# The first quad's softmax in two halves of 256 columns, with a new table of order and other counts of filler matmuls

## The chip, the core and the metric

The kernel runs on one core of one Trainium2 chip. Its time is device microseconds (us) of that core for one launch. Three runs of the kernel before gave a median of 709.91 us (709.32 to 710.12).

A core has TensorE (PE in the rows; PEld is its weight load), VectorE (DVE), ScalarE (ACT), GpSimd (POOL) and SyncE (SP), which here only issues transfers. A "q" behind a name (SPq) is an engine's sequencer. Each engine works through its own list in order and waits on semaphores for the others.

## The reference

Attention between 512 tokens and 32 state rows in each of 32 heads, in both directions, then two MLPs over the 2176 rows that come out, all in float32:

```python
scores = scale * x @ state.T                 # per head: x 512x64, state 32x64
a = softmax(scores);  xread = a @ state      # (a /= sum + 1e-09)
a2 = softmax(scale * state @ x.T);  sread = a2 @ x
x = concatenate([xread, sread], axis=2)      # heads side by side: 512 wide
h = x @ w_in;  g = where(h >= 1, h, where(h <= -1, 0, (h + 1) ** 2 / 4))
x = g @ w_out                                # first MLP, 2048 wide
return (x @ w_a * (x @ w_b)) @ w_out         # second MLP, 1536 wide
```

The weights arrive as 64-bit numbers and are brought to float32 on the chip.

## The kernel before

**Stages.** The first stage computes the attention and the first half of the first MLP; the second, h = g @ w_out in a seven-product scheme over quarter blocks; the third, the second MLP in the same scheme. Every large product is computed from operands that are split into a high and a low part, as three matmuls on a pair of 128-row blocks (`three`, L407). The stage around the change lasts until some 140 us; its matmuls and nearly all others are issued on line L401 (`mms`).

**The first stage.** Heads are taken four at a time: a "quad" is four heads, and a pair of quads is one of the four batches. For quad k, `a_qk` (L631) multiplies scores into bank 4 or 5 (in the rows `first`, later one tile `lower`), for quad 0 in two halves of 256 columns as its tokens land. `a_soft` (L655) is the softmax in eleven steps, each on 512 columns: transpose and maximum on DVE, subtraction on POOL, exponential on ACT, sum, a small addition and the reciprocal on DVE, multiplication on POOL, transpose back on DVE, the high part on ACT (`hi_of`, L381) and the low part on DVE (L683). The other direction is `s_soft` (L736), `s_tr` (L783: transposes on TensorE) and `s_read` (L802: the product with the tokens `xn`, 32 small matmuls for each quad, quad 0 first).

**State times weights.** Instead of attention times state and then times w_in, state times w_in is computed once for each batch and each quarter n of w_in (`w_steps`, L694; PE line L704 into the tile `upper`), then split by one copy on ACT (L376) and one subtraction on DVE (L386). After that one **unit** of six matmuls of 512 columns (`h_mm`, L853) gives 128 of the 2048 hidden columns for one batch. Units 0 to 3 of batch 0 use quarter 0, units 4 to 7 quarter 1, and so on. A `gate` (L829: two ACT steps, one of them at times on POOL, and DVE at L847) turns a unit into g, which is stored to DRAM.

**Weights.** Each pair of blocks of w_in is 1 MB as loaded (`conv_steps`, L420). It is turned into float32 by three steps, each on DVE, POOL or ACT: copy (L451 on ACT, L453 elsewhere), byte (L457 on ACT, L459 elsewhere) and join (L470, always DVE).

**What sets the order.** All this is recorded as a list of operations. `Flow.order` (L98) then lists them with assumed durations and due times; the table `NUDGE` (L20) shifts single operations' due times by numbers, and takes an engine from some. SP issues the loads in that order, and they are carried in one queue. The start alone is written out by hand, in `phase_one`: after `s0` and `s1`, the steps of quads 0 and 1, a row of named steps whose order on DVE, ACT and POOL is kept (`flow.row`).

**Fillers.** A filler is a 128 by 128 float32 matmul of a constant, whose result is not used (L908). Ten of zeros stand at the start (`WARM`), ten ahead of the first state product and ten behind it (`FILL`), and `Flow.order` puts some ahead of operations that begin a bank anew, when by its own reckoning PE would be idle after the first 13 us (`SPAN`).

Of the kernel before, what the change touches and what calls it, by code (L numbers as in the profile page):

```python
# [9 lines left out]
F32 = mybir.dt.float32  # L10
# [7 lines left out]


NUDGE = {  # L20
    2: (-37,), 44: (39,), 49: (0.5, "POOL"), 68: (160.5,), 74: (20,), 91: (-0.5,), 99: (24.5, "POOL"), 100: (13,),
    105: (18,), 110: (33,), 118: (94.5,), 133: (10.5,), 134: (17,), 135: (32,), 146: (2413,), 187: (27, "POOL"),
    219: (0, "POOL"), 260: (2,), 316: (2,), 790: (-14.5,), 1015: (-9,), 1070: (-7,), 1097: (1,), 1105: (-3.5,),
    1110: (2,), 1142: (-7,), 1215: (3,), 1229: (-7.5,), 1248: (2,), 1257: (-2,),
}


class Flow:
# [9 lines left out]
    DMA_FROM = 1.1  # L38

    EARLY, SOON = 26.0, 0.3  # L40
    FULL, SPARE, FILLER, SPAN = 0.75, 0.4, 0.23, (13.0, 60.0)

    def __init__(self):
        self.ops = []
        self.last = {}
        self.readers = {}
        self.loose = set()
        self.gate = None
        self.hold = None
# [5 lines left out]
        self.fresh, self.fill = set(), {}  # L55
        self.psum = {}

    def op(self, engs, emit, rd=(), wr=(), size=0, loose=False, port=False):
        i = len(self.ops)
        if port:  # L60
            self.port.add(i)
        self.hurry[i] = self.rush
        if loose:
            self.loose.add(i)
        self.psum[i] = {b - b % 2 if b > 3 else b for s, lo, hi in [*rd, *wr] if s == "P" for b in range(lo, hi)}
        deps = set()
        last, readers = self.last, self.readers
# [12 lines left out]
        for c in cells(list(wr) + shut):  # L80
            if c in last:
                deps.add(last[c])
            deps.update(readers.pop(c, ()))
            last[c] = i
        if self.gate is not None and size:
            deps.add(self.gate)
        if self.hold is not None:
            deps.add(self.hold)
        e = next(iter(engs))
        if self.row is not None and len(engs) == 1 and e in ("DVE", "ACT", "POOL"):  # L90
            if e in self.row:
                deps.add(self.row[e])
            self.row[e] = i
        deps.discard(i)
        self.ops.append((engs, emit, sorted(deps), size))
        return i

    def order(self):  # L98
# [101 lines left out]
        for i in use:  # L200
            if self.ops[i][4] != "PE" or start[i] > self.SPAN[1]:
                continue
            best = (0, 0)
            for b in (0, 1, 2, 3, 4, 6):
                on = [x for x in use if b in self.psum[x]]
                at = next((k for k, x in enumerate(on) if (start[x], x) >= (start[i], i)), None)
                if at is not None and on[at] in self.fresh:
                    t = max([f] + [fin[x] for x in on[:at]])
                    best = max(best, (int(self.FULL * (start[i] - t - self.SPARE) / self.FILLER), b))
            if best[0] > 0 and start[i] > self.SPAN[0]:  # L210
                self.fill[i] = best
# [6 lines left out]
def attention_then_two_mlps(  # L218
# [13 lines left out]
    nc = tc.nc  # L232
# [136 lines left out]
    def eng(e):  # L369
        return {"DVE": nc.vector, "POOL": nc.gpsimd}[e]  # L370
# [278 lines left out]
    def g32(t):  # L649
        return t.rearrange("p (a n) -> p a n", n=NS)  # L650

    def b32(t):
        return t.unsqueeze(2).to_broadcast([P, 16, NS])

    def a_soft(k, sub=("POOL",), mult=("POOL",), low=("DVE", "POOL")):  # L655
        d = qs[k]
        t1, b = d["t1"], sbank[k]
        mx, sm = d["sm"].sub(16, 16), d["sm"].sub(32, 16)
        hi, lo = att[k]

        def spread(engs, alu, v):
            op(
                {x: {"DVE": 0.7, "POOL": 1.05}[x] for x in engs},
                lambda e: eng(e).tensor_tensor(g32(t1()), g32(t1()), b32(v()), alu),
                regs(t1, v),
                regs(t1),
                port=True,
            )

        return [  # L670
            lambda: op({"DVE": 0.72}, lambda e: nc.vector.transpose(t1(), banks[b]), [bank(b)], regs(t1)),
            lambda: op({"DVE": 0.69}, lambda e: nc.vector.reduce_max(mx(), g32(t1()), axis=AX.X), regs(t1), regs(mx)),
            lambda: spread(sub, ALU.subtract, mx),
            lambda: act(t1, t1, 512, AF.Exp, regs(t1), regs(t1), scale=SCALE),
            lambda: op({"DVE": 0.69}, lambda e: nc.vector.reduce_sum(sm(), g32(t1()), axis=AX.X), regs(t1), regs(sm)),
            lambda: plus_tiny(mx, d["sm"].sub(32, 32), 16),
            lambda: op({"DVE": 0.25}, lambda e: nc.vector.reciprocal(mx(), mx()), regs(mx), regs(mx)),
            lambda: spread(mult, ALU.mult, mx),
            lambda: op({"DVE": 0.71}, lambda e: nc.vector.transpose(d["at"](), t1()), regs(t1), regs(d["at"])),
            lambda: hi_of(hi, d["at"], 512, regs(d["at"]), regs(hi)),  # L680
            lambda: op(
                {x: {"DVE": t_tt(512), "POOL": 1.05}[x] for x in low},
                lambda e: eng(e).tensor_tensor(lo(), d["at"](), hi(F32), ALU.subtract),  # L683
                regs(d["at"], hi),
                regs(lo),
                port=True,
            ),
        ]
# [721 lines left out]
    def phase_one():  # L1410
# [23 lines left out]
        tr, mx, sub, exp, sm, eps, rec, mult, back, high, low = range(11)  # L1434
        copy, byte, join = range(3)
        prod, top, rest, top1, rest1 = range(5)
        warm(FILL[0])
# [233 lines left out]
```

## Time and profile before

| | |
|---|---|
| median of three runs | 709.91 us (709.32 to 710.12) |
| profiled execution, its own time | 709.89 us |
| its span, first to last instruction | 708.1 us |
| PE busy | 697.8 us, 99% of the span |
| DVE, ACT, POOL busy | 554.6, 419.1, 110.2 us |
| moved by DMA | 128.93 MB |

What follows comes from that one execution; 1.8 us of its own time lie outside of the span. The page's share of an engine is a mean over all stages. "The chain that ended last" is followed from the last instruction back, at each step to what released it. In a timeline row the number in brackets is how long the engine had been idle, and the arrow names what ended that.

### The profile page before, as it was taken

To read this page: it belongs to the slowest core of one execution; us is meant where nothing else is said; L and a number is where in the kernel's file an instruction comes from. 1 tells how busy PE (TensorE), PEld (TensorE's weight loads), DVE (VectorE), ACT (ScalarE), POOL (GpSimd) and SP (SyncE) were. 2 spreads that over 40 slices of the span, in tenths; PEclk is the share of its full clock that TensorE was granted. 3 is DMA by queue.
4 is the path that set the end of the run, shared out by engine and by line. 5 is a ranking of instruction groups with operands and counts; after the bars stand their busy time and mean duration, and the time that the engine had idled before them with its cause. 6 is when DMAs were issued, how large, how long until landed. Compare 5 with 4: busy or idle time off the path is not lost.

```text
span 708.1 us, 12274 instructions
## 1 busy us (share of the span) xinstructions
PE 697.8 (99%) x4834; PEld 657.1 (93%) x4834; DVE 554.6 (78%) x702; ACT 419.1 (59%) x626; POOL 110.2 (16%) x76
## 2 busy tenths in 40 slices
PE   7899999999999999999999999999999999999998
PEld 6666677989999999999999999999999999999998
DVE  7897898899996787899998686756636889986761
ACT  5689888787444455666576576465325545544440
POOL 3564858873000000000000000000000000000000
PEclk9999999999999999999999999999999999999999
DMA  8978879596583165151445767362731358454201
GB/s 311 407 254 308 290 260 293 166 321 202 193 285 118 63 198 189 48 192 65 135 149 180 239 223 245 120 222 76 235 112 42 98 156 286 141 161 138 87 32 45
DMA packets 75994, 128.93 MB, mean 182 GB/s; under 512 B 5664, under 2 KB 52000, under 8 KB 75936
## 3 DMA queue, kind: packets, MB, share of 16 engines
q1 hardware_dynamic: 75664, 128.01, 53.8%
q8 instruction: 38, 0.62, 0.4%
q14 instruction: 20, 0.16, 0.1%
q10 hardware_dynamic: 272, 0.13, 0.1%
HBM read 84.87 MB, written 43.25 MB: 181 GB/s over the span
## 4 chain that ended last, share of the span: by engine, by line
PE 93%; DMA 3%; DVE 3%; issue 0%; ACT 0%; SPq 0%; ACTq 0%; DVEq 0%
PE bank L401 86%; PE bank L885 2%; PE upper L704 2%; DMA fs<-in_xn_dram 2%; DMA fs<-in_xt_dram 1%; PE lower L812 1%; DMA f<-in_w_dram 1%; PE first L812 0%; DVE f L964 0%; DVE r L386 0%; PE lower L791 0%; DVE fs L470 0%; PE lower L581 0%; DVE rh L386 0%; ACT rh L376 0%
## 5 line engine op out<-in xcount | busy, mean ns | idle before, releaser
L401 PE MATMUL bank<-rh,r 128*128 128x352 f32 (+2 forms) x1398 | 222.6, 315 | 0.0
L401 PEld LDWEIGHTS bank<-rh,r 128*128 128x128 f32 x1398 | 215.8, 189 | 1.0 <-DVE rh L386 0.7
L376 ACT ACTIVATE f<-bank 128x368 f32<-128x368 f32 (+3 forms) x183 | 82.6, 453 | 124.9 <-PE bank L401 122.9
L401 PE MATMUL bank<-r,r 128*128 128x368 f32 (+1 forms) x960 | 156.2, 315 | 0.0
L401 PEld LDWEIGHTS bank<-r,r 128*128 128x128 f32 x960 | 147.9, 188 | 0.0
L376 ACT ACTIVATE rh<-f 128x736 fp32r<-128x736 f32 (+5 forms) x120 | 100.4, 846 | 72.3 <-PE bank L401 62.4
L386 DVE TENSOR_TENSOR f<-bank,f 128x368 f32<-128x368 f32 (+2 forms) x170 | 86.1, 514 | 70.7 <-PE bank L401 59.7
L386 DVE TENSOR_TENSOR rh<-f,rh 128x736 fp32r<-128x736 f32 (+5 forms) x120 | 117.0, 984 | 28.2 <-ACT rh L376 28.0
L401 PE MATMUL bank<-r 128*128 128x512 f32 (+1 forms) x582 | 119.4, 358 | 0.4 <-DVE r L683 0.4
L401 PEld LDWEIGHTS bank<-r 128*128 128x128 f32 x582 | 94.6, 189 | 24.6 <-issue 4.2
L386 DVE TENSOR_TENSOR r<-f,r 128x768 fp32r<-128x768 f32 (+6 forms) x85 | 96.0, 1139 | 16.4 <-ACT r L376 16.0
L376 ACT ACTIVATE r<-f 128x768 fp32r<-128x768 f32 (+6 forms) x85 | 80.2, 953 | 37.5 <-PE bank L401 17.3
L401 PE MATMUL bank<-rh 128*128 128x352 f32 (+2 forms) x564 | 93.4, 318 | 0.2 <-DVE f L386 0.2
L964 DVE TENSOR_TENSOR f<-f 128x256 f32<-128x256 f32 (+7 forms) x108 | 86.4, 818 | 6.9 <-DMA f<-p_d 4.9
L401 PEld LDWEIGHTS bank<-rh 128*128 128x128 f32 x564 | 88.4, 189 | 1.4 <-issue 0.5
L401 PE MATMUL bank<-r,rh 128*128 128x368 f32 (+1 forms) x480 | 80.3, 315 | 0.0
L401 PEld LDWEIGHTS bank<-r,rh 128*128 128x128 f32 x480 | 74.3, 188 | 0.0
L451 ACT ACTIVATE f<-f 128x512 fp8e5<-128x512 fp8e5 (+1 forms) x31 | 32.2, 1040 | 23.4 <-DMA f<-in_w_dram 17.9
L470 DVE SCALAR_TENSOR_TENSOR f<-f 128x1024 uint32<-128x1024 uint32 (+1 forms) x34 | 36.5, 1072 | 6.4 <-ACT f L457 6.4
L457 ACT ACTIVATE f<-f 128x512 fp8e5<-128x512 f32 (+1 forms) x35 | 37.3, 1067 | 0.7 <-POOL f L453 0.3
L833 ACT ACTIVATE f<-bank,half 128x512 f32<-128x512 f32 x40 | 27.1, 683 | 7.3 <-PE bank L401 3.1
L842 POOL TENSOR_TENSOR f<-f 128x512 f32<-128x512 f32 x20 | 27.5, 1384 | 22.4 <-ACT f L833 16.9
(76 smaller groups left out, 438.8 us busy)
## 6 DMA issues: line engine op xcount, KB each, us to landing
f<-in_w_dram SPq DMA_DIRECT2D x25, 1024.0 KB, 6.2
f<-g_d SPq DMA_DIRECT2D x36, 368.0 KB, 5.0
f<-p_d SPq DMA_DIRECT2D x17, 768.0 KB, 5.1
g_d<-f SPq DMA_DIRECT2D x40, 256.0 KB, 4.2
f<-in_w_dram SPq DMA_DIRECT2D x18, 512.0 KB, 4.1
p_d<-f SPq DMA_DIRECT2D x48, 184.0 KB, 2.1
g_d<-fs SPq DMA_DIRECT2D x28, 256.0 KB, 4.8
f<-g_d SPq DMA_DIRECT2D x16, 352.0 KB, 4.9
```

What stands on the lines that cost most here:

```text
L376: lambda e: nc.scalar.activation(dst(), src(), func, **{k: (v() if callable(v) else v) for k, v in kws.items()}),
L386: op({"DVE": t_tt(n)}, lambda e: nc.vector.tensor_tensor(dst(), a(), b(), alu), rd, wr, port=port)
L401: nc.tensor.matmul(o, w, x, start=first and k == 0, stop=last and k == n - 1, skip_group_check=onto)
L451: nc.scalar.activation(to(), of(), AF.Copy, saturate=False)
L457: nc.scalar.activation(to(), z(), AF.Copy, saturate=False)
L470: lambda e: nc.vector.scalar_tensor_tensor(out(U32), words_of(1, U32)(), 5, z(U32), ALU.logical_shift_right, ALU.bitwise_or),
L704: nc.tensor.matmul(banks[ab[q]][o : o + NS, :cols].rearrange("p (f x) -> p f x", x=P), st[q]()[64 * h : 64 * h + 64, NS * j : NS * j + NS] ...
L812: nc.tensor.matmul(banks[4][64 * e2 : 64 * e2 + 64, o : o + NS], xn()[:, c * 256 + p * 128 + e2 * 64 : c * 256 + p * 128 + (e2 + 1) * 64], ...
L833: lambda e: nc.scalar.activation(g(), h(), AF.Relu, bias=half[:, 0:1], scale=0.5),
L842: eng(e).tensor_tensor(g(), g(), g(), ALU.mult)
L885: nc.tensor.matmul(banks[b][:, P * i : P * i + P], w[:, P * c : P * c + P], xs()[:, P * c : P * c + P], start=c == 0, stop=c == 3,)
L964: lambda e: eng(e).tensor_tensor(dst(), a(), b(), alu),
```

## The change

`a_soft` takes a `part`: with 0 or 1 it does steps one to ten on 256 of the 512 columns (8 groups of 32 in place of 16), and only the low part stays whole. Quad 0 is done in two such parts; the second half has small vectors of its own. The row of steps in `phase_one` is written anew. Two fillers less stand at the start (8), two more ahead of the first state product (12), and three are put ahead of the first `s_read` (`awake`); fillers by reckoning are now allowed from 8 us on. The table `NUDGE` has other entries throughout, which moves operations in all stages.

```diff
 NUDGE = {
-    2: (-37,), 44: (39,), 49: (0.5, "POOL"), 68: (160.5,), 74: (20,), 91: (-0.5,), 99: (24.5, "POOL"), 100: (13,),
...
+    3: (21,), 18: (23,), 20: (39,), 21: (31.5,), 59: (5.5, "POOL"), 61: (-5,), 66: (-4.5,), 74: (41.5,), 76: (42,),
...
-    FULL, SPARE, FILLER, SPAN = 0.75, 0.4, 0.23, (13.0, 60.0)
+    FULL, SPARE, FILLER, SPAN = 0.75, 0.4, 0.23, (8.0, 60.0)
...
+        for i, (k, b) in self.awake.items():
+            self.fill[i] = max(self.fill.get(i, (0, b))[0], k), self.fill.get(i, (0, b))[1]
...
-    WARM, BETWEEN = 10, 1
+    WARM, BETWEEN = 8, 1
...
-    FILL = (10, 10)
+    FILL = (12, 10)
...
-    def a_soft(k, sub=("POOL",), mult=("POOL",), low=("DVE", "POOL")):
+    def a_soft(k, sub=("POOL",), mult=("POOL",), low=("DVE", "POOL"), part=None):
...
+        n, full, hi0 = 512, at, hi
+        if part is not None:
+            n = 256
+            t1, at, hi = (v.sub(n * part, n) for v in (t1, at, hi))
+            src = lambda: banks[sbank[k]][:, n * part : n * part + n]
+        m = n // NS
...
+            if b + q == 0:
+                flow.awake[len(flow.ops)] = (3, 4)
             op({"PE": 1.1}, emit, regs(xn, a2t), [bank(4)], loose=True)
...
-        s0 = a_soft(0, ("POOL",), ("POOL",), ("DVE",))
+        s0 = [a_soft(0, ("POOL",), ("POOL",), ("DVE",), h) for h in range(2)]
...
-            s0[tr], s0[mx], s0[sub], s1[tr], s1[mx], s1[sub], c0[copy], s0[exp], c0[byte], s1[exp], s0[sm], c0[join],
-            s0[eps], s0[rec], s0[mult], v0[prod], lambda: warm(FILL[1]), c1[copy], v0[top], v0[top1], c1[byte],
-            s1[sm], s1[eps], s1[rec], s1[mult], v0[rest], v0[rest1], s0[back], s0[high], s1[back], s1[high], s0[low],
-            c2[copy], s1[low], c1[join], c2[byte],
+            *first[:exp], *last[:exp], *s1[:exp], first[exp], last[exp], c0[copy], *first[sm:back], *last[sm:back],
+            c0[byte], s1[exp], c0[join], first[back], first[high], v0[prod], lambda: warm(FILL[1]), c1[copy],
+            last[back], last[high], v0[top], v0[top1], c1[byte], *s1[sm:back], v0[rest], v0[rest1], s1[back],
+            s1[high], last[low], c2[copy], s1[low], c1[join], c2[byte],
```

The lines from `a_soft` on stand lower in the changed file: L376, L386, L401, L457 and L704 are there L378, L388, L403, L459 and L726.

**DVE at the start.** Before, from the first transpose to the first join of weights (`fs<-f`); names are the tiles, `first_91` the scores of quad 0 and `first_92` those of quad 1:

```order
L671 STREAM_TRANSPOSE fs<-first_91 128x512
L672 TENSOR_REDUCE fs<-fs 128x16
L751 TENSOR_REDUCE fs<-first_91 128x1
L671 STREAM_TRANSPOSE fs<-first_92 128x512
L751 TENSOR_REDUCE fs<-first_92 128x1
L672 TENSOR_REDUCE fs<-fs 128x16
L675 TENSOR_REDUCE fs<-fs 128x16
L470 SCALAR_TENSOR_TENSOR fs<-f_66 128x512
```

And in the changed kernel:

```order
L693 STREAM_TRANSPOSE fs<-first_91 128x256
L694 TENSOR_REDUCE fs<-fs 128x8
L693 STREAM_TRANSPOSE fs<-first_91 128x256
L694 TENSOR_REDUCE fs<-fs 128x8
L693 STREAM_TRANSPOSE fs<-first_92 128x512
L694 TENSOR_REDUCE fs<-fs 128x16
L773 TENSOR_REDUCE fs<-first_91 128x1
L773 TENSOR_REDUCE fs<-first_92 128x1
L697 TENSOR_REDUCE fs<-fs 128x8
L686 TENSOR_REDUCE fs<-fs 128x8
L699 RECIPROCAL fs<-fs 128x8
L697 TENSOR_REDUCE fs<-fs 128x8
```

The join, the last row before, comes four rows further on, behind the sums and reciprocals of both halves.

**ACT around the state product of quarter 1.** Before, from the first `s_read`'s copy on (`first_91` 128x4x32); `upper` 128x2x512 is the high part of that product, `f_66` 128x1024 the byte step of a pair of weights:

```order
L376 ACTIVATE fs<-first_91 128x4x32
L376 ACTIVATE r_65<-upper 128x256 x2
L457 ACTIVATE f_66<-f_66 128x1024
L376 ACTIVATE r_65<-upper 128x2x512
L457 ACTIVATE f_66<-f_66 128x1024
L833 ACTIVATE f_66<-bank_69,half 128x512
```

And in the changed kernel:

```order
L378 ACTIVATE fs<-first_91 128x4x32
L378 ACTIVATE r_65<-upper 128x256 x2
L459 ACTIVATE f_66<-f_66 128x1024 x2
L378 ACTIVATE r_65<-upper 128x2x512
L857 ACTIVATE f_66<-bank_69,half 128x512
```

The second byte step now stands ahead of the high part.

**PE from the first `s_read` on.** Before (`first_91<-fs` is `s_read`, `lower` the next batch's scores, a bank x6 one unit, `ident` a filler):

```order
L812 MATMUL first_91<-fs 64x32 x32
L704 MATMUL upper<-fs 32x256 x8
L581 MATMUL lower<-fs 32x512 x8
L704 MATMUL upper<-fs 32x512 x8
L401 MATMUL bank_69<-r_65 128x512 x6
L401 MATMUL bank_70<-r_65 128x512 x6
L401 MATMUL bank_67<-r_65 128x512 x6
L401 MATMUL bank_68<-r_65 128x512 x6
L704 MATMUL upper<-fs 32x512 x8
L401 MATMUL bank_69<-r_65 128x512 x6
L908 MATMUL bank_67<-ident 128x128 x2
L704 MATMUL upper<-fs 32x512 x8
```

And in the changed kernel, from `s_read`'s three fillers on:

```order
L932 MATMUL first_91<-ident 128x128 x3
L834 MATMUL first_91<-fs 64x32 x32
L726 MATMUL upper<-fs 32x256 x8
L583 MATMUL lower<-fs 32x512 x8
L726 MATMUL upper<-fs 32x512 x8
L403 MATMUL bank_69<-r_65 128x512 x6
L403 MATMUL bank_70<-r_65 128x512 x6
L932 MATMUL bank_68<-ident 128x128 x2
L403 MATMUL bank_67<-r_65 128x512 x6
L403 MATMUL bank_68<-r_65 128x512 x6
L726 MATMUL upper<-fs 32x512 x8
L403 MATMUL bank_69<-r_65 128x512 x6
```

Behind this the changed list has one more unit (bank_70), one filler and the state product that ends the excerpt of before: eight units stand ahead of it in place of seven. The product after that one follows four units later in place of seven.

## Rows read from the trace of the kernel before

**Rows 1.** The page, busy time, share of the span and count of each engine

```profile
PE 697.8 (99%) x4834; PEld 657.1 (93%) x4834; DVE 554.6 (78%) x702; ACT 419.1 (59%) x626; POOL 110.2 (16%) x76
```

**Rows 2.** What PE waited for, whole span: us in total, times, longest

```profile
PE first L812 <- DMA fs<-in_xn_dram: 1.8, 1, 1.8
PE upper L704 <- DVE fs L470: 1.2, 1, 1.2
PE upper L704 <- DVE r L386: 1.2, 2, 0.8
```

**Rows 3.** The chain that ended last: start us, us, what; stretch 9 to 62 us

```profile
9.97 13.78 DMA fs<-in_xn_dram
...
23.88 3.47 PE first L812 x64
...
30.79 1.16 DVE fs L606
...
33.74 2.48 DVE fs L470 x2
36.22 0.60 DVE f L847
36.82 1.14 DVE fs L609
...
37.99 0.23 DVE fs L546
...
38.24 0.35 DVE fs L611
38.59 0.57 DVE fs L847
39.16 1.14 DVE r L386
...
40.35 1.09 PE upper L704 x16
41.44 9.74 PE bank L401 x42
...
61.38 1.99 PE lower L812 x64
```

**Rows 4.** Windows, PE only: us, PE busy (x), granted clock, DMA share, GB/s

```profile
22.00:24.00 2.00, 0.23 (x6) 1.00 1.04 414
...
24.50:27.50 3.00, 3.00 (x62) 0.50 1.02 407
```

**Rows 5.** Timeline 7 to 43 us: start us, us, engine, line, op, tiles [idle before]

```profile
7.44 0.72 DVE L671 STREAM_TRANSPOSE fs<-first 128x512 f32<-128x512 f32 x1 [3.48 <-PE first L639]
...
9.44 2.50 PE L908 MATMUL bank<-ident 128*128 128x128 f32 x20
...
18.79 0.77 DVE L453 COPY f<-f 128x1024 uint8<-128x1024 uint8 x1
...
19.70 2.19 POOL L459 CAST f<-f 128x1024 fp8e5<-128x1024 f32 x1 [2.62 <-ACT fs L774]
...
20.97 1.52 DVE L453 COPY f<-f 128x1024 uint8<-128x1024 uint8 x1
```

**Rows 6.** Timeline, a later stretch of the same, 29.5 to 41 us

```profile
29.52 1.24 DVE L605 STREAM_TRANSPOSE fs<-lower 128x1024 f32<-128x1024 f32 x1
...
30.30 1.37 POOL L453 COPY f<-f 128x1024 uint8<-128x1024 uint8 x1 [1.19 <-DMA f<-in_w_dram]
...
30.85 1.03 ACT L376 ACTIVATE r<-upper 128x1024 fp32r<-128x1024 f32 x1 [0.34 <-PE upper L704]
31.77 1.38 ACT L457 ACTIVATE f<-f 128x1024 fp8e5<-128x1024 f32 x1
...
32.52 1.22 DVE L386 TENSOR_TENSOR r<-upper,r 128x1024 fp32r<-128x1024 f32 x1
```

More of the change, by code (lines that the diff above doesn't have):

```diff
@@ L20 @@
 NUDGE = {
-    2: (-37,), 44: (39,), 49: (0.5, "POOL"), 68: (160.5,), 74: (20,), 91: (-0.5,), 99: (24.5, "POOL"), 100: (13,),
-    105: (18,), 110: (33,), 118: (94.5,), 133: (10.5,), 134: (17,), 135: (32,), 146: (2413,), 187: (27, "POOL"),
-    219: (0, "POOL"), 260: (2,), 316: (2,), 790: (-14.5,), 1015: (-9,), 1070: (-7,), 1097: (1,), 1105: (-3.5,),
-    1110: (2,), 1142: (-7,), 1215: (3,), 1229: (-7.5,), 1248: (2,), 1257: (-2,),
+    3: (21,), 18: (23,), 20: (39,), 21: (31.5,), 59: (5.5, "POOL"), 61: (-5,), 66: (-4.5,), 74: (41.5,), 76: (42,),
+    77: (33,), 78: (87,), 83: (33.5,), 87: (30.5,), 171: (8, "POOL"), 173: (4.5,), 199: (7,), 251: (2.5,),
+    271: (2.5,), 275: (-5.5,), 415: (2.5,), 1080: (-7,), 1100: (9,), 1110: (3.5,), 1117: (-2.5,), 1118: (2.5,),
+    1152: (-4,), 1173: (-2,), 1258: (1.5,),
 }
@@ L54, in __init__ @@
         self.nudge = {}
-        self.fresh, self.fill = set(), {}
+        self.fresh, self.fill, self.awake = set(), {}, {}
         self.psum = {}
@@ L653, in b32 @@
         return t.unsqueeze(2).to_broadcast([P, 16, NS])
-    def a_soft(k, sub=("POOL",), mult=("POOL",), low=("DVE", "POOL")):
+    def a_soft(k, sub=("POOL",), mult=("POOL",), low=("DVE", "POOL"), part=None):
         d = qs[k]
-        t1, b = d["t1"], sbank[k]
-        mx, sm = d["sm"].sub(16, 16), d["sm"].sub(32, 16)
+        t1, at, src = d["t1"], d["at"], lambda: banks[sbank[k]]
+        small = d["sm"] if part != 1 else bs[0]["sm"]
         hi, lo = att[k]
+        n, full, hi0 = 512, at, hi
[4 more added lines that the diff above has]
+        m = n // NS
+        mx, sm = small.sub(16, m), small.sub(32, m)
+        held = [bank(sbank[k])]
         def spread(engs, alu, v):
             op(
-                {x: {"DVE": 0.7, "POOL": 1.05}[x] for x in engs},
-                lambda e: eng(e).tensor_tensor(g32(t1()), g32(t1()), b32(v()), alu),
+                {x: {"DVE": 0.165 + n / 960, "POOL": 0.18 + 0.0017 * n}[x] for x in engs},
+                lambda e: eng(e).tensor_tensor(
+                    g32(t1()), g32(t1()), v().unsqueeze(2).to_broadcast([P, m, NS]), alu
+                ),
                 regs(t1, v),
@@ L668, in spread, with plus @@
             )
+        def plus():
+            v = small.sub(32, 32)
+            op(
+                {"DVE": 0.09 + 0.0022 * m},
+                lambda e: nc.vector.reduce_sum(mx(), v().rearrange("p (t a) -> p a t", t=2)[:, :m], axis=AX.X),
+                regs(v),
+                regs(mx),
+            )
+        t = 0.16 + n / 960
         return [
-            lambda: op({"DVE": 0.72}, lambda e: nc.vector.transpose(t1(), banks[b]), [bank(b)], regs(t1)),
-            lambda: op({"DVE": 0.69}, lambda e: nc.vector.reduce_max(mx(), g32(t1()), axis=AX.X), regs(t1), regs(mx)),
+            lambda: op({"DVE": t + 0.02}, lambda e: nc.vector.transpose(t1(), src()), held, regs(t1)),
+            lambda: op({"DVE": t}, lambda e: nc.vector.reduce_max(mx(), g32(t1()), axis=AX.X), regs(t1), regs(mx)),
             lambda: spread(sub, ALU.subtract, mx),
[L674 to L677, printed above, removed]
+            lambda: act(t1, t1, n, AF.Exp, regs(t1), regs(t1), scale=SCALE),
+            lambda: op({"DVE": t}, lambda e: nc.vector.reduce_sum(sm(), g32(t1()), axis=AX.X), regs(t1), regs(sm)),
+            plus,
+            lambda: op({"DVE": 0.16 + 0.006 * m}, lambda e: nc.vector.reciprocal(mx(), mx()), regs(mx), regs(mx)),
             lambda: spread(mult, ALU.mult, mx),
-            lambda: op({"DVE": 0.71}, lambda e: nc.vector.transpose(d["at"](), t1()), regs(t1), regs(d["at"])),
-            lambda: hi_of(hi, d["at"], 512, regs(d["at"]), regs(hi)),
+            lambda: op({"DVE": t + 0.01}, lambda e: nc.vector.transpose(at(), t1()), regs(t1), regs(at)),
+            lambda: hi_of(hi, at, n, regs(at), regs(hi)),
             lambda: op(
                 {x: {"DVE": t_tt(512), "POOL": 1.05}[x] for x in low},
-                lambda e: eng(e).tensor_tensor(lo(), d["at"](), hi(F32), ALU.subtract),
-                regs(d["at"], hi),
+                lambda e: eng(e).tensor_tensor(lo(), full(), hi0(F32), ALU.subtract),
+                regs(full, hi0),
                 regs(lo),
@@ L1436, in phase_one @@
         prod, top, rest, top1, rest1 = range(5)
+        first, last = s0
         warm(FILL[0])
         for f in (
-            s0[tr], s0[mx], s0[sub], s1[tr], s1[mx], s1[sub], c0[copy], s0[exp], c0[byte], s1[exp], s0[sm], c0[join],
-            s0[eps], s0[rec], s0[mult], v0[prod], lambda: warm(FILL[1]), c1[copy], v0[top], v0[top1], c1[byte],
-            s1[sm], s1[eps], s1[rec], s1[mult], v0[rest], v0[rest1], s0[back], s0[high], s1[back], s1[high], s0[low],
-            c2[copy], s1[low], c1[join], c2[byte],
+            *first[:exp], *last[:exp], *s1[:exp], first[exp], last[exp], c0[copy], *first[sm:back], *last[sm:back],
+            c0[byte], s1[exp], c0[join], first[back], first[high], v0[prod], lambda: warm(FILL[1]), c1[copy],
+            last[back], last[high], v0[top], v0[top1], c1[byte], *s1[sm:back], v0[rest], v0[rest1], s1[back],
+            s1[high], last[low], c2[copy], s1[low], c1[join], c2[byte],
         ):
```

## The prediction

> **What bounds the kernel now.** I read the page first, then the waits of PE, the chain that ended last, the granted clock, and the timeline of the first 45 us. PE is busy 99% of the span [rows 1], so time can only come from its idle time, its fillers and its slow stretches. Nearly all of the idle time lies early: 1.8 us before the first `s_read`, which waits for the tokens `xn`, 1.2 us before the first state product, 1.2 us in two waits of `upper` for DVE [rows 2]. From 40.35 us on the chain is a row of PE pieces to the end of the first stage and nearly to the end of the kernel. So what the change is worth can be read at one point: the state product at 40.35 us, with seven units done ahead of it (the list of PE in the section on the change). A unit costs PE 9.74 / 42 x 6 = 1.39 us [rows 3].
>
> Two things set that point. First, one queue of transfers runs full: DMA share over 1.0 and 410 GB/s [rows 4], and the pieces land one after another at that rate. The first `xn` lands at 9.97 + 13.78 = 23.75 us and `s_read` starts at 23.88 [rows 3]; a pair of weights lands just before POOL takes it at 30.30, after 1.19 us of waiting for it [rows 6]. Second, DVE: from 30.79 to 40.30 the chain is DVE without a gap worth naming [rows 3].
>
> The clock belongs here too. From 22 to 24 us PE was busy for 0.23 of 2 us at a granted 1.00; then the grant fell to 0.50 (1.2 of 2.4 GHz) for the stretch of `s_read` [rows 4], which took 3.47 us, where the same 64 records take 1.99 us at full clock [rows 3]. That is 1.48 us which the new fillers may save.
>
> **The change part by part.**
>
> *Halves.* A transpose of 512 columns takes 0.72 us and one of 1024 takes 1.24 [rows 5, 6], so the fixed part is 2 x 0.72 - 1.24 = 0.20 us. Four full-width steps of quad 0 on DVE become eight: +0.8 us. The small steps (addition, reciprocal) become four; the trace has one small addition at 0.23 and one reciprocal at 0.35, both twice as wide as a whole quad's [rows 3], so +0.2 to +0.6. I take +1.2 us of DVE in all (0.8 to 1.4). The halves overlap POOL and ACT with DVE, but they don't begin earlier: the first transpose waits for the scores of the whole quad, the second for nothing of its own. And the first join of weights, for which the first state product waited 1.2 us [rows 2], now stands behind both halves' sums. So PE's first two units come later by about what DVE has to do more, 1.2 us (bounds: 0 if the overlap pays for it, 2.0 if the join's delay adds up with it).
>
> *Fillers.* Twenty filler records took 2.50 us [rows 5], so a filler of two records costs 0.25 us. Two more behind the second scores stand in a wait. The three ahead of `s_read`, 0.75 us, stand in the wait for `xn`: PE was done at 23.88 - 1.8 = 22.1 us [rows 2, 3], now 22.1 + 1.2 + 0.75 = 24.1.
>
> *`s_read` starts later.* The new table swaps the two `xn` loads: the half that quad 0 needs is issued second. One load is 0.52 MB, at 410 GB/s 1.28 us, so it lands at 23.75 + 1.28 = 25.03 us and `s_read` starts at 25.1 in place of 23.9. That covers PE's 24.1 with 1 us to spare, so the halves and the fillers cost nothing at this point, and they gain nothing either. With the clock kept, `s_read` ends at 25.1 + 2.0 = 27.1, against 23.88 + 3.47 = 27.35: a gain of 0.25 us only. From its end to the end of DVE's maximum (30.79 + 1.16) was 4.60 us; now that is 31.7. One join follows in DVE's list, 2.48 / 2 = 1.24 us [rows 3], so DVE is free for the low part of quarter 1 at 32.9.
>
> *ACT's list.* That low part needs the high part, which before ran at 30.85 [rows 6], between two byte steps of weights (the list of ACT in the section on the change). Now both byte steps stand ahead of it, and the second waits for the pair of weights that lands at some 30.2. As many bytes stand before that pair in SP's queue as before, so its landing stays. From the trace [rows 6]: POOL's copy 30.30 + 1.37 = 31.67; ACT's byte step 31.77 + 1.38 = 33.15; high part + 1.03 = 34.18; DVE's low part + 1.22, with small gaps at 35.4. In the kernel before it ended at 32.52 + 1.22 = 33.74. DVE is free at 32.9, so it waits 1.3 us, and whatever `s_read` gained is lost in that wait. PE waits as well: it needs the low part for the third matmul of unit 4.
>
> *From there to the point.* DVE then has, by its new list: a join 1.24, a gate 0.60, the sum 1.14, the addition and reciprocal 0.23 + 0.35 (0.62 with their gaps), three gates of some 0.6 (1.8) and the low part of quarter 2, 1.14 [rows 3]. Together 6.54 us, to 35.4 + 6.5 = 41.9. PE starts the state product for which `upper` must be free at 41.95. It has done eight units by then, one more than before, worth 1.39 us: 41.95 - 1.39 = 40.56 against 40.35 us. The change is 0.2 us **late** at this point.
>
> *Behind it.* The product after that one now comes four units later, at 41.95 + 1.1 + 4 x 1.39 = 48.6 us (a state product took 1.09 us [rows 3]). It needs the last join of weights. DVE has ahead of its end a copy (0.77 to 1.52 us [rows 5]), a transpose 1.24, two gates 1.2, a join 1.24, a low part 1.14 and that join 1.24: 6.8 to 7.6 us from 41.9, so 48.7 to 49.5. PE waits 0.1 to 0.9 us; I take 0.3, near the lower end, since DVE's chain from 30.79 to 40.30 had hardly any gaps [rows 3]. The other moves of the table, in later stages, are between neighbours on DVE and ACT while PE is the chain; I cost them at 0, with 0.2 us either way, for what is near the edge there.
>
> **Sum:** 709.89 (the profiled execution, 0.02 under the median) + 0.2 + 0.3 = 710.4 us.
>
> **The rivals.**
>
> *The clock gain comes through* (faster). If the weights' byte step doesn't hold the high part (a landing 1.3 us earlier, or POOL and ACT that much quicker), DVE goes on at 32.9 and all behind it is 1.3 us earlier: 40.56 - 1.3 = 39.3 against 40.35, and the wait at 48.6 goes. 709.9 - 1.1 = 708.8 us, 708.3 if the gates behind it close up as well. For it: the 1.48 us of slow clock are real, and 0.7 to 1.2 us of waits for DVE [rows 2] stand right there. Against it: the queue is full, so nothing in it can land earlier.
>
> *DVE and POOL hold each other up* (slower). Alone, a copy of 1024 on DVE took 0.77 us; beside POOL's cast, which ran from 19.70 to 21.89 and itself took 2.19 in place of some 1.37 [rows 6], the same copy took 1.52 [rows 5]. So one collision costs 0.75 to 0.8 us. The stretch from 34 to 49 us has no slack on DVE, and its joins and copies meet POOL's in another order than before. Two collisions more there than the sum holds make 710.4 + 1.5 = 711.9 us. It decides from two on; one alone stays inside the forecast. The Trainium skill (SBUF — State Buffer, section "SBUF: two separate sides") says that DVE and GpSimd share one pair of ports as a lock held for a whole instruction, so that the loser blocks fully instead of sharing. The trace agrees nearly: the copy began at 20.97, and POOL's end at 21.89 + 0.77 would be 22.66, against a measured end of 20.97 + 1.52 = 22.49. By that rule a collision could cost up to a whole POOL instruction, 1.37 us, and two of them 710.4 + 2.7 = 713.1 us.
>
> *The clock is not kept* (slower, but little). With 8 fillers at the start PE is idle before the first scores and again until the second; if the grant rises late, PE's row of eighteen fillers runs at half clock. PE then comes to `s_read` up to 1 us later, inside its slack. If the grant falls again during `s_read`, that ends at 28.6 and DVE is free at 34.4 in place of 32.9, 0.2 us after the high part: 710.6 us.
>
> **How the numbers follow.** A measurement of this kernel tells 0.2% (1.4 us) from no change; faster is below 708.5, slower above 711.3. Forecast 0.62: 0.59 within, 0.03 above. Clock gain comes through 0.18: half of it under 708.5. Collisions 0.12, above. Clock not kept 0.08, within. So faster 0.09, same 0.76, slower 0.15. Of the range, the lower end 709.0 takes in the forecast less its 0.2 us each for the late table, the wait at 48.6 and the halves, and the upper part of the first rival; the upper end 712.0 takes in the collisions.
>
> **What would show it.** In the profile of the changed kernel: the first `s_read` starting near 25.1 us and taking 2.0 us; the granted clock at 1.00 from 20 to 30 us; ACT's high part of quarter 1 ending near 34.2, behind the byte step; PE idle for 1 to 2 us between 33 and 35.4; the state product with eight units ahead of it near 42 us, and a short wait near 48.6. It is wrong if that product starts before 41 us (the first rival) or after 43 (collisions), or if PE has new waits behind 60 us.

## The result, and the profile after

| | kernel before | changed kernel |
|---|---|---|
| median of five runs | 709.36 us (709.32 to 710.12) | 713.01 us (712.61 to 713.62) |
| ratio | 1 | 1.0052 (95%: 1.0040 to 1.0064) |
| profiled execution, its span | 708.1 us | 711.0 us |

The change costs 0.5%. The forecast was 710.4 us, with a range up to 712.0, so it was wrong, and on the slow side. Each later run stands beside runs of the kernel before on the same chip (their medians lie from 708.6 to 709.3 us), so ratios are what to compare; 0.1% is 0.7 us.

The page of the changed kernel, first line, which answers [rows 1]; PE is busy 99% in both, so the loss is not to be read from shares:

```profile
PE 700.9 (99%) x4858; PEld 658.9 (93%) x4858; DVE 557.5 (78%) x709; ACT 418.6 (59%) x626; POOL 115.8 (16%) x79
```

Waits of PE over the whole span (us in total, times, longest), which answer [rows 2]:

```profile
PE upper L726 <- DVE r L388: 2.5, 2, 1.7
PE first L641 <- DMA fs<-in_xt_dram: 2.4, 2, 1.6
```

The waits for tokens and for the first join are gone. In their place PE waits longer for its first scores, and once for 1.7 us for a low part (L388). The timeline of PE (start, us, what, in brackets idle before it) shows where:

```profile
24.45 0.83 PE L932 MATMUL first<-ident 128*128 128x128 f32 x6
25.21 2.06 PE L834 MATMUL first<-fs 128*64 128x32 f32 x64
...
34.84 2.57 PE L403 MATMUL bank<-r 128*128 128x512 f32 x10 [0.38 <-DVE r L388]
...
41.54 1.09 PE L726 MATMUL upper<-fs 64*32 64x512 f32 x16
...
48.35 1.09 PE L726 MATMUL upper<-fs 64*32 64x512 f32 x16
```

```profile
61.28 2.06 PE L834 MATMUL lower<-fs 128*64 128x32 f32 x64
65.07 1.09 PE L726 MATMUL upper<-fs 64*32 64x512 f32 x16 [1.73 <-DVE r L388]
```

Up to the end of the second batch's `s_read` the two executions are level: 61.28 + 2.06 = 63.34 us here, 61.38 + 1.99 = 63.37 in [rows 3]. Then PE stands still for 1.73 us in a place where the kernel before goes straight on. The chain that ended last (start, us, what) leads from that wait back to a load:

```profile
50.99 8.70 DMA f<-in_w_dram
...
59.84 1.36 POOL f L455
61.20 1.98 POOL f L866 x2
...
63.80 1.23 DVE r L388
...
65.07 1.09 PE upper L726 x16
```

(The second row is the copy L455 and the third the squares L866.) POOL's timeline shows what is queued there:

```profile
55.11 1.04 POOL L866 TENSOR_TENSOR f<-f 128x512 f32<-128x512 f32 x1 [0.88 <-ACT f L857]
59.84 1.36 POOL L455 COPY f<-f 128x1024 uint8<-128x1024 uint8 x1 [3.68 <-DMA f<-in_w_dram]
61.13 2.04 POOL L866 TENSOR_TENSOR f<-f 128x512 f32<-128x512 f32 x2
```

DVE's next gate shows how long it stood, and ACT's row of the kernel before shows where the copy was then:

```profile
62.20 0.69 DVE L871 SCALAR_TENSOR_TENSOR f<-f,bank 128x512 f32<-128x512 f32 x1 [5.32 <-POOL f L866]
```

```profile
62.00 1.37 ACT L451 ACTIVATE f<-f 128x1024 fp8e5<-128x1024 fp8e5 x1
```

POOL has a copy of weights (L455) in its list ahead of two squares of gates (L866). The copy waits 3.68 us for its load, the squares stand behind it, DVE's two gates need the squares, and the low part that PE needs stands behind the gates in DVE's list. In the kernel before, this copy was ACT's, at 62.00 us, since the old table took it from POOL; the new table doesn't.

### The profile page after: what moved, and what is told of

The parts are those of the page before. It is cut to its first block, busy times and chain, and to the rows that moved or that the text cites. A ratio compares the mean times of both kernels' runs of the same rounds, so it can differ in the third digit from the quotient of the medians.

```text
span 711.0 us, 12328 instructions
## 1 busy us (share of the span) xinstructions
PE 700.9 (99%) x4858; PEld 658.9 (93%) x4858; DVE 557.5 (78%) x709; ACT 418.6 (59%) x626; POOL 115.8 (16%) x79
## 4 chain that ended last, share of the span: by engine, by line
PE 87%; DMA 5%; DVE 4%; POOL 1%; ACT 1%; issue 1%; SPq 0%; DVEq 0%; ACTq 0%; POOLq 0%
PE bank L403 81%; DMA f<-in_w_dram 3%; PE bank L909 2%; PE upper L726 2%; PE bank L932 1%; DMA fs<-in_xt_dram 1%; DVE f L988 1%; DMA f<-g_d 1%; DVE rh L388 1%; DVE r L388 1%; PE lower L834 1%; DVE fs L871 1%; DVE f L472 0%; POOL fs L601 0%; DVE fs L472 0%
## 5 line engine op out<-in xcount | busy, mean ns | idle before, releaser
L403 PE MATMUL bank<-rh,r 128*128 128x352 f32 (+2 forms) x1398 | 222.5, 315 | 0.0
L403 PEld LDWEIGHTS bank<-rh,r 128*128 128x128 f32 x1398 | 215.8, 189 | 0.8 <-DVE rh L388 0.5
L403 PE MATMUL bank<-r,r 128*128 128x368 f32 (+1 forms) x960 | 156.3, 315 | 0.1
L378 ACT ACTIVATE f<-bank 128x368 f32<-128x368 f32 (+3 forms) x183 | 82.5, 454 | 118.6 <-PE bank L403 117.2
L403 PEld LDWEIGHTS bank<-r,r 128*128 128x128 f32 x960 | 147.8, 188 | 0.4 <-ACT f L378 0.4
L378 ACT ACTIVATE rh<-f 128x736 fp32r<-128x736 f32 (+5 forms) x120 | 100.6, 846 | 73.7 <-PE bank L403 64.4
L388 DVE TENSOR_TENSOR f<-bank,f 128x368 f32<-128x368 f32 (+2 forms) x170 | 86.7, 516 | 72.4 <-PE bank L403 59.8
L388 DVE TENSOR_TENSOR rh<-f,rh 128x736 fp32r<-128x736 f32 (+5 forms) x120 | 116.7, 981 | 28.5 <-ACT rh L378 28.1
L403 PE MATMUL bank<-r 128*128 128x512 f32 (+1 forms) x582 | 120.0, 358 | 0.4 <-DVE r L388 0.4
L403 PEld LDWEIGHTS bank<-r 128*128 128x128 f32 x582 | 94.4, 189 | 25.7 <-issue 3.4
L388 DVE TENSOR_TENSOR r<-f,r 128x768 fp32r<-128x768 f32 (+6 forms) x85 | 96.9, 1152 | 14.9 <-ACT r L378 14.7
L378 ACT ACTIVATE r<-f 128x768 fp32r<-128x768 f32 (+6 forms) x85 | 80.3, 953 | 40.0 <-PE bank L403 17.0
L403 PE MATMUL bank<-rh 128*128 128x352 f32 (+2 forms) x564 | 93.6, 318 | 0.3 <-DVE f L388 0.3
L403 PEld LDWEIGHTS bank<-rh 128*128 128x128 f32 x564 | 88.3, 189 | 1.7 <-DVE f L388 0.7
L403 PE MATMUL bank<-r,rh 128*128 128x368 f32 (+1 forms) x480 | 80.6, 315 | 0.1
L403 PEld LDWEIGHTS bank<-r,rh 128*128 128x128 f32 x480 | 74.2, 188 | 0.4 <-DVE rh L388 0.4
L459 ACT ACTIVATE f<-f 128x512 fp8e5<-128x512 f32 (+1 forms) x34 | 36.0, 1057 | 2.7 <-POOL f L455 1.3
L871 DVE SCALAR_TENSOR_TENSOR f<-f,bank 128x512 f32<-128x512 f32 x40 | 26.6, 677 | 9.3 <-POOL f L866 6.9
```

What stands on the lines that cost most here:

```text
L378: lambda e: nc.scalar.activation(dst(), src(), func, **{k: (v() if callable(v) else v) for k, v in kws.items()}),
L388: op({"DVE": t_tt(n)}, lambda e: nc.vector.tensor_tensor(dst(), a(), b(), alu), rd, wr, port=port)
L403: nc.tensor.matmul(o, w, x, start=first and k == 0, stop=last and k == n - 1, skip_group_check=onto)
L459: nc.scalar.activation(to(), z(), AF.Copy, saturate=False)
L871: lambda e: nc.vector.scalar_tensor_tensor(g(), g(), 1.0, h(), ALU.min, ALU.max),
```

## The experiments

In the diffs `put(i, j)` takes operation i out of the order and sets it right behind operation j; nothing else moves.

**The copy ahead of the squares.** First the copy (229) goes behind the second square (252):

```diff
     order = flow.order()
+    put(229, 252)
```

> The changed kernel; on POOL alone one copy of weights stands behind the two gate squares that followed it. In the changed kernel that copy began at 59.84 us after 3.68 us of waiting for its load, and the two squares ran behind it (61.13 to 63.17). Theory Q (the squares are held in POOL's list by the late load): the squares run as soon as ACT has their input, DVE's gates and the low part behind them follow, the low part starts near 60.7 in place of 63.80, PE's wait of 1.7 us before its state product at 65.07 is gone, and the time falls from 713.0 by 1.7 to about 711.3 us. Rival L (the late load itself is what PE waits for, wherever the copy stands): the wait only moves to the next product that needs that pair, and the time stays above 712.5 us.

Measured: ratio 1.0032 (1.0021 to 1.0043), 710.98 against 708.61 us. PE has no wait in the stretch from 40 to 80 us, and POOL runs the squares at once:

```profile
56.93 1.04 POOL L866 TENSOR_TENSOR f<-f 128x512 f32<-128x512 f32 x1 [1.16 <-ACT f L857]
58.15 1.04 POOL L866 TENSOR_TENSOR f<-f 128x512 f32<-128x512 f32 x1 [0.19 <-ACT f L857]
59.14 1.37 POOL L455 COPY f<-f 128x1024 uint8<-128x1024 uint8 x1
```

The copy starts no later than it did, so its place ahead of the squares gained nothing. Theory Q holds, with 0.2% (1.4 us); by the two intervals that is 0.04 to 0.36%. 0.3% is left.

Then the load of that pair of weights (228) goes out ahead of the small state load (219) and a store (207):

```diff
     order = flow.order()
+    put(219, 228)
+    put(207, 228)
```

> The changed kernel; in SP's list alone the load of that pair of weights stands ahead of the small state load (128 KB) and of one store (256 KB) that were issued just ahead of it. The load can't be issued before about 50.9 us, since a unit on PE frees its place. If the two transfers ahead of it in the queue made it late, it lands 0.9 us (0.38 MB at 410 GB/s) to 3 us (the queue carried 193 and 57 GB/s from 52 to 54 us) earlier than 59.69 us, and PE's wait of 1.7 us falls by as much: 710.9 to 712.1 us. If not, it lands at 59.5 us or later and the time stays near 713.0. Theory Q takes either; it says that the wait falls by what the landing gains.

Measured: 1.0031 (1.0018 to 1.0043).

```profile
56.80 1.36 POOL L455 COPY f<-f 128x1024 uint8<-128x1024 uint8 x1 [0.20 <-DMA f<-in_w_dram]
```

The load went out at 50.36 us and POOL began the copy at 56.80, after a wait of only 0.20 us, 3.0 us earlier than before the edit; the wait near 63 us was gone. So the landing was late because of what went ahead of it in the one queue, and either remedy is enough.

**A second place, near 377 us.** In the profile after, PE fell back by another 0.7 us there against the profile before, behind a join that stood later in DVE's list:

```diff
     order = flow.order()
+    put(1225, 1222)
+    put(1226, 1223)
+    put(1227, 1312)
+    put(1259, 1228)
```

> The changed kernel; in the third stage alone (356 to 362 us) one sum, the high and low part of it and the join of a pair of weights stand in DVE's and ACT's lists as they did before the change. In the changed kernel that join started at 362.06, the load behind it was issued at 362.05, 2.9 us later than before when the later start of all is taken off, ACT waited 1.54 us for it and PE lost 0.7 us near 377. Theory: with the join back, the load goes out near 359.5, ACT doesn't wait, PE's loss of 0.7 us is gone: 712.3 us. Rival: the loss near 377 has another cause (the order of the gates there) and stays: 713.0.

Measured: 1.0046 (1.0032 to 1.0061), which can't be told from the unedited 1.0052. Both edits together:

> The first and the third of these edits together. If both waits are single and apart, the gains add up: 713.0 - 1.7 - 0.7 = 710.6 us, 1.2 us over the kernel before. What is then left is what the change does besides these two waits. If the two gains don't add up (one hides the other, or new waits come up), 711.3 or more.

Measured: 1.0034 (1.0023 to 1.0045), as the first alone. And in a second execution of the changed kernel (below) the loss near 377 us was not there at all. I had taken a chance delay of one execution for an effect of the list.

**How far does one execution speak?**

> The kernel before once more, unchanged, for its trace. In the first four runs the times of the kernel before lay at 707.7 to 710.3 us (median 708.6), and the profiled execution of it that was read first took 709.89. Theory C: the fall of the granted clock in the stretch of the first s_read is not there in every execution; in one without it s_read takes 2.0 us in place of 3.47 and the state product that started at 40.35 us starts about 1 us earlier, and the time is near 708.5 us. Rival: the clock falls each time and the spread comes from later waits; then s_read takes 3.4 to 3.5 us again.

> The same again, for a second trace: by theory C s_read takes 2.0 us in at least one of the two.

> The changed kernel once more, for a second trace and a ratio on the same chip. The waits of 1.7 us near 63 us and of 0.7 us near 377 us are due to the lists of POOL and DVE, so they are there again within 0.6 us, and the ratio is 1.005 again. If they came from chance in the landing of loads, one or both is missing.

The changed kernel: 1.0052 again (1.0030 to 1.0074), single runs from 709.9 to 717.0 us. The wait near 63 us was there (1.30 us; 0.60 in the third experiment, which leaves that place alone), so its place is regular and its length is not. The kernel before took 708.1 and 709.4 us in the two executions. Windows of the second one, PE only (us, PE busy, granted clock, DMA share, GB/s), and its `s_read`:

```profile
22.00:24.00 2.00, 0.72 (x25) 1.00 1.03 410
24.00:26.00 2.00, 1.93 (x46) 0.67 1.02 408
26.00:28.00 2.00, 2.00 (x38) 0.50 1.03 414
```

```profile
23.28 2.97 PE L812 MATMUL first<-fs 128*64 128x32 f32 x64 [1.54 <-DMA fs<-in_xn_dram]
```

The clock fell in all three executions of the kernel before that were read, to 0.50, so neither of these two runs bears out the first half of theory C; a later run with the same start does (the reverse run under "Start or table?"). It fell at another moment of `s_read`, which took 3.47, 2.37 and 2.97 us. And the state product that stood at 40.35 us in [rows 3] started at 39.52 and 39.60 us: the execution on which the sum was built was 0.8 us late at this very point.

**What is the clock worth?** Three fillers ahead of the first `s_read` of the kernel before:

```diff
     order = flow.order()
+    k, b = flow.fill.get(120, (0, 4))
+    flow.fill[120] = max(k, 3), b
```

> The kernel before with one edit: three filler matmuls stand on PE ahead of the first s_read, 0.75 us in a wait of 1.8 us. If the fillers keep the clock, s_read takes 2.0 us and ends 1.4 us earlier whenever the clock would have fallen; DVE's chain from 29 to 40 us then starts up to 1.4 us earlier. Theory C: since not every execution of the kernel before has the fall, the mean gain is below 1 us: ratio 0.9985 to 1.000. Rival (the fall is there each time and its 1.48 us come through): ratio 0.998.

Measured: 0.9999 (0.9990 to 1.0009). The granted clock stayed at 1.00 and `s_read` was done at 25.97 us, but the state product started at 39.61 us, as without fillers. DVE shows why. Its two joins (L470), first in this kernel, then in the second execution of the kernel before:

```profile
32.29 3.21 DVE L470 SCALAR_TENSOR_TENSOR fs<-f 128x1024 uint32<-128x1024 uint32 x2
35.42 0.68 DVE L847 SCALAR_TENSOR_TENSOR f<-f,bank 128x512 f32<-128x512 f32 x1
```

```profile
32.92 2.57 DVE L470 SCALAR_TENSOR_TENSOR fs<-f 128x1024 uint32<-128x1024 uint32 x2
35.41 0.68 DVE L847 SCALAR_TENSOR_TENSOR f<-f,bank 128x512 f32<-128x512 f32 x1
```

They begin 0.63 us earlier, take 0.64 us longer, and end at the same moment. While the first of them runs, POOL does its subtraction:

```profile
30.07 1.36 POOL L453 COPY f<-f 128x1024 uint8<-128x1024 uint8 x1 [1.21 <-DMA f<-in_w_dram]
31.36 1.92 POOL L599 TENSOR_TENSOR fs<-fs 128x1024 f32<-128x1024 f32 x1
```

It ends at 33.28 us here and at 33.27 in the other execution, and the joins end 2.22 us behind it in both. POOL's subtraction did not gain from the earlier `s_read`, since it stands right behind a copy that waited for its load. So in this execution a load held DVE by way of POOL.

**Start or table?** The changed kernel up to what it places before 44 us, and then all other operations in the order and on the engines of the kernel before:

```diff
     order = flow.order()
+    tail = [
...
+    ]
+    order = order[: len(order) - len(tail)] + tail
+    for i, e in {205: 'ACT', 229: 'ACT', 266: 'POOL', 230: 'ACT', 291: 'POOL', 300: 'ACT', 342: 'POOL', 280: 'POOL', 296: 'ACT', 405: 'ACT', 425: 'POOL', 439: 'ACT', 484: 'ACT', 422: 'POOL', 505: 'DVE', 672: 'POOL', 681: 'ACT'}.items():
+        flow.ops[i] = (*flow.ops[i][:4], e)
```

The last two lines give 17 operations the engine of the kernel before; 229 is the copy of above.

> The changed kernel up to the operations that its table places before 44 us (its start, its fillers, its softmax in halves); all operations behind that stand in the order, and on the engines, of the kernel before. Theory T (the start costs 0.5 us and the rest of the loss comes from the later part of the table): +0.5 us, ratio 1.0007 (0.9995 to 1.002). Rival S (the start is to blame: it hands over at another moment, and the waits follow from that): ratio 1.004 or more.

Measured: 1.0012 (1.0003 to 1.0021). The same the other way round:

> The reverse: the kernel before up to what it places before 44 us, and behind that the order and the engines of the changed kernel. Theory T: the loss is here, +3 us, ratio 1.0043 (1.003 to 1.0055), with PE's wait near 63 us. Rival S: ratio 0.999 to 1.001.

Measured: 1.0055 (1.0041 to 1.0068), but not through the same place: behind the old start, the new list makes PE wait 1.90 us near 48 us for a join, and none near 63 us. The clock fell behind that wait:

```profile
49.30 1.09 PE L704 MATMUL upper<-fs 64*32 64x512 f32 x16 [1.90 <-DVE fs L470]
```

```profile
50.00:52.00 2.00, 2.00 (x13) 0.66 0.48 164
52.00:54.00 2.00, 2.00 (x6) 0.50 0.70 188
```

This run shows that the new list loses without the new start, not what it loses with it. Its start is that of the kernel before, and there the clock did not fall:

```profile
23.32 2.32 PE L812 MATMUL first<-fs 128*64 128x32 f32 x64 [1.80 <-DMA fs<-in_xn_dram]
```

```profile
24.00:26.00 2.00, 1.93 (x64) 1.00 1.02 406
```

So the fall is not in every execution, as theory C had it. It matters little: the state product of 39.5 us started at 39.29 us here. With the border at 140 us:

> The changed kernel up to what it places before 140 us (all of the first stage), then the order of the kernel before. If all of the later loss lies in the first stage: ratio 1.005. If, as the traces of single executions have it, some 1.2 us of it near 63 us and 0.4 us between 66 and 200 us are regular and the rest comes from the second and third stage: +0.5 + 1.2 + 0.4 = 2.1 us, ratio 1.003.

Measured: 1.0043 (1.0028 to 1.0058). The profiled execution was a long one (714.0 us), and shows what the wait can bring on. PE near 63 us, then windows of the stretch:

```profile
65.60 1.85 PE L726 MATMUL upper<-fs 64*32 64x512 f32 x16 [1.84 <-DVE r L388]
```

```profile
64.00:66.00 2.00, 0.40 (x8) 0.95 0.61 229
66.00:68.00 2.00, 2.00 (x24) 0.50 1.01 305
68.00:70.00 2.00, 2.00 (x20) 0.70 0.99 394
```

After 1.84 us without work the clock fell to 0.50 (1.2 of 2.4 GHz), and the state product took 1.85 us in place of 1.09. From the start of `s_read` to that of the state product after this one it took 11.75 us (61.70 to 73.45), where the kernel before took 8.19 (61.31 to 69.50): 3.6 us more, about twice the wait. After the waits of 1.73 and 1.30 us the clock held. With the copy behind the squares as well:

> The changed first stage, the old order behind 140 us (ratio 1.0043), and on POOL the copy of weights behind the two gate squares. Theory Q: the wait near 63 us, with the fall of the clock that followed it in one execution (granted 0.50 from 66 us, 1.7 us more), is what the first stage loses behind its start: ratio 1.0043 - 0.0031 = 1.0012, and in any case below 1.0025. If the first stage has other losses of the size, it stays at 1.003.

Measured: 1.0019 (1.0009 to 1.0028). So the copy takes 0.24%, 1.7 us, of the first stage (0.06 to 0.42% by the two intervals).

**The halves.** Quad 0's softmax in one piece (each step of the first half does nothing, each of the second does all 512 columns):

```diff
+            one = lambda f: f if part else lambda e: None
...
+                lambda: op({"DVE": t}, one(lambda e: nc.vector.reduce_max(MX(), g32(T1()), axis=AX.X)), regs(t1), regs(mx)),
...
+                lambda: op({"DVE": t + 0.01}, one(lambda e: nc.vector.transpose(AT(), T1())), regs(t1), regs(at)),
```

> The changed kernel with quad 0's softmax in one piece of 512 columns: each step of the first half does nothing, each of the second half does all, in the same place of every list. The forecast costed the halves at nothing, since s_read waits for its tokens until 25.1 us. If so, the first units come earlier by up to 1.2 us, s_read starts at 25.0 to 25.3 us all the same, and the ratio is that of the changed kernel, 1.005. If the halves gain through the overlap, s_read or the state product at 41.5 us comes later without them and the time grows by 0.5 us or more; if their extra work on DVE costs, it falls by 0.5 or more.

Measured: 1.0045 (1.0030 to 1.0061), not to be told from 1.0052. `s_read` started at 24.67 us, below the 25.0 that I expected, directly behind its three fillers; PE's own work and not the tokens set its start in this execution.

**What of the start costs?** On the form with the border at 44 us, the high part (105) ahead of the second byte step (152):

```diff
     order = flow.order()
+    put(152, 105)
```

> The kernel with the changed start and the old list behind 44 us (ratio 1.0012), with one edit on ACT: the high part of quarter 1 stands ahead of the second byte step, as before the change. The forecast said that the byte step holds the high part and with it DVE. In the run of the unedited form the high part started at 32.15 us, right behind the byte step, and DVE was idle from 32.03 to 33.18 us. If that is the step, the high part starts near 29.7 and the low part near 32.0, 1.1 us earlier, the state product of 41.16 us comes up to 1.1 us earlier, and the ratio falls to 0.9997 (0.999 to 1.0005). Rival (DVE's joins then run beside POOL's spread, as with the fillers alone, and take the gain): the product comes at most 0.4 us earlier, ratio 1.0007 to 1.0015.

Measured: 1.0017 (1.0008 to 1.0026), no gain. The low part did come at 32.18 in place of 33.18 us, and the state product at 40.42 in place of 41.16. Then DVE's copy ran beside POOL, and PE waited. DVE and PE of the edited form:

```profile
40.28 2.17 DVE L455 COPY f<-f 128x1024 uint8<-128x1024 uint8 x1
```

```profile
47.05 3.24 PE L403 MATMUL bank<-r 128*128 128x512 f32 x13 [1.18 <-DVE f L871]
```

and of the unedited form:

```profile
40.70 1.47 DVE L455 COPY f<-f 128x1024 uint8<-128x1024 uint8 x1
```

```profile
46.78 3.48 PE L403 MATMUL bank<-r 128*128 128x512 f32 x14 [0.18 <-DVE f L871]
```

Of the 1.0 us, 0.6 went into a join that took 1.81 in place of 1.22 us, beside a subtraction of POOL. The copy took the rest. POOL was at its next subtraction from 39.90 to 41.82 us, and the copy ended 0.63 us behind it; in the unedited form the copy ended 0.64 us behind the same subtraction (41.53). So here, too, the times say that POOL set when DVE was done. By the Trainium skill (SBUF — State Buffer, section "SBUF: two separate sides"), GpSimd and a DVE instruction that needs the pair of ports they share take it as a lock: the one that comes later is held until the other's instruction is done. The copy alone takes 0.77 us [rows 5], so the estimate by that rule is 41.82 + 0.77 = 42.59; the measured end is 42.45, so the trace nearly agrees. The token loads in the old order:

```diff
     order = flow.order()
+    put(87, 86)
```

> The same form with one edit on SP instead: the two token loads stand in the order of before, the one that quad 0 needs first. s_read may then start up to 1.2 us earlier, near 23.2 us, but its second half needs the other load and can't end before 25.9 us. By the forecast's own chain the byte step behind it is bound by the weights that land near 29.5 us, so DVE and the state product don't move: ratio 1.0012 again (1.0003 to 1.002). If the later s_read is what the start costs: 0.4 us off, 1.0006.

Measured: 1.0014 (1.0005 to 1.0023), no gain. Both edits:

> Both edits. If the high part is what the start costs and the loads are free: as with the high part alone, 0.9997. If each gives something: 0.999 or less, which would be faster than the kernel before.

Measured: 1.0012 (1.0003 to 1.0021). No form of the new start was faster than the kernel before.

## Why the prediction was wrong

**Right in its times, the start.** `s_read` at 25.1 us with 2.0 us: 25.21 and 2.06. The clock at 1.00 from 20 to 30 us: so it was. The high part behind the byte step: it ended at 33.53 (forecast 34.2). PE waited 0.38 us beside fillers of 0.60, less than the 1 to 2 us forecast. The state product behind eight units: 41.54 (41.95). The one after: 48.35 (48.6), directly behind the unit before it, where a wait of 0.3 was forecast. The halves are worth nothing: no difference in the time was found. The swapped loads are worth nothing: none was found either. The clock gain is swallowed: 0.9999. For the start the sum had +0.2 us at the state product, +0.5 with the later wait; the run with the old list behind it gives 0.12%, 0.2 to 1.5 us.

**Partly by luck, the way there.** The forecast had `s_read` start when its tokens land, with PE done 1 us before. In the profile of the changed kernel it followed its fillers without a wait. The chain that ended last (start, us, what) there leads back over the fillers to the first scores, and on to 41 us by way of POOL:

```profile
10.09 4.35 PE bank L932 x24
...
24.61 0.67 PE first L932 x6
25.28 1.99 PE first L834 x64
...
31.91 2.83 POOL fs L601
34.76 2.00 POOL fs L866
```

So the fillers, costed at nothing because they stand in a wait, were on the chain of this execution. No run takes them out of the changed start, and what they cost there stays open. With the old list behind 44 us the chain is the forecast one: the load of weights landed at 29.36 us, and POOL's copy, ACT's byte step and high part and DVE's low part followed.

**Right by luck, the baseline.** That the start stands level at 63.3 us in the first two profiles comes from the execution of the kernel before, which was 0.8 us late at the point that I chose. The sum began there. Less the one unit more, the state product stood at 41.54 - 1.39 = 40.15 us: 0.2 us early against 40.35, as the first execution has it, and 0.6 late against 39.52 and 39.60. The total was hardly touched, since the term that failed is far larger.

**Wrong, one sentence.** It reads: "The other moves of the table, in later stages, are between neighbours on DVE and ACT while PE is the chain; I cost them at 0, with 0.2 us either way". It was mis-sized at 0 where the runs have 0.52 - 0.12 = 0.40%, some 2.8 us (0.25 to 0.55% by the two intervals). 1.4 to 1.7 us of it is the copy on POOL. The moves were not between neighbours, nor on DVE and ACT alone: 17 operations behind 44 us changed their engine, and one of them, a copy, stood on POOL ahead of two squares, with its load behind a small load and a store. I had followed the new lists to 49 us and then let "PE is the chain" stand for the rest. But PE is the chain only as long as the engines ahead of it are in time, and the list of POOL that shows the copy ahead of the squares was there to be read. My own test, new waits of PE behind 60 us, is what it failed.

**The rivals.** The collisions were named as the slow side, with 711.9 us. DVE and POOL did hold each other up, and that ate the gain of two experiments, but the loss itself is a load that holds a list. The clock gain did not come through. My reason was that the queue is full; the runs show how that reaches DVE: joins and copies that start earlier run beside a subtraction of POOL and end when they did, and with the fillers alone POOL's subtraction stood right behind a copy that had waited for its load. (The 1.37 us that the prediction gives for POOL's cast is the row of a copy; the trace has the cast alone at 1.35 us.)

**Open.** What in the start costs its 0.12% was not found: neither the high part nor the loads. Behind 140 us some 0.1% seems to be lost (1.0052 against 1.0043, and 1.0032 against 1.0019 with the copy moved), with intervals that overlap. No place was found for it: the waits of 0.2 to 1.25 us near 264 and 273 us come and go from one execution to the next, in the kernel before too (0.22 and 0.50 us), and the loss near 377 us stood in one execution alone.

## What to carry to other kernels

When a table moves operations everywhere, walk every engine's list to the end of the stage and stop at each instruction that waits for a transfer: what is queued behind it, and who needs that. A kept clock is worth what the next engine in line can use of it, so ask what else that engine waits for, and which operation the earlier work will run beside. Look at a second execution before building a sum on a start time or a wait of one.

## What the runs showed of the hardware

The same 1 MB load took 8.70 us from issue to landing behind a 128 KB state load and a 256 KB store (7.6 to 8.8 us in the eight executions with that order), and 6.3 us in the one execution where it went out ahead of both. So the place in the queue is worth some 1.3 to 2.5 us; 0.6 of the 3.0 us above is the earlier issue. What went ahead of it is slow for its size. Whether it was the small load or the store, no run separates. From 52 to 54 us the queue was 0.66 busy and moved 125 GB/s (61 to 175 in those eight, 236 with the load first), where it moves 410 GB/s when full of large loads:

```profile
52.00:54.00 2.00, 2.00 (x16) 1.00 0.66 125
```

A wait of PE can cost twice its length. After 1.84 us without work the clock fell to 0.50, and 1.7 us more were lost; after 1.90 us, in the run with the old start and the new list, it fell too, and the next state product came after 6.97 us in place of 5.33. The length of the wait alone does not tell: the clock also fell after 1.54 us (the second execution of the kernel before), and it stayed at 1.00 after waits of 1.30, 1.73 and 1.80 us. This may be why single runs of the changed kernel spread from 709.9 to 717.0 us, but only two profiles show a fall behind a wait that the new list made.
